# Fences between outputs and crosses: an instruction without operation in place of a copy, one per group in place of two

## The chip, the cores and the metric

The kernel runs on one core of one Trainium2 chip. The metric is the device time in microseconds of one execution, as the median of several runs. The five engines of the core each take their instructions in order from a queue of their own: TensorE (matmuls and weight loads; PE and PEld in the profile), VectorE (DVE), ScalarE (ACT), GpSimd (POOL) and SyncE (SP, which issues DMAs). They wait for each other through semaphores.

## The reference

A retention layer (linear attention with a decay per head) is followed by one wide layer with a swish.

```python
scores = scale * np.matmul(q, k.transpose(0, 1, 3, 2))       # q, k, v: 8 x 8 x 576 x 64, f32
gamma = 1.0 - 2.0 ** (-5.0 - np.arange(H, dtype=np.float32))
Dmat = np.where(rel >= 0, gamma[:, None, None] ** rel[None, :, :], 0.0)
attn = np.matmul(scores * Dmat[None, :, :, :], v)
x = attn.transpose(0, 2, 1, 3).reshape(B * S, H * D)         # 4608 x 512
h = x @ w_in                                                 # w_in: 512 x 2048
out = (h * (1.0 / (1.0 + np.exp(-beta * h)))) @ w_out        # w_out: 2048 x 512
```

## The kernel before

The 576 rows of a batch are cut into 512 rows, in four chunks of 128, and a tail of 64; the eight tails make a ninth block. The retention is computed chunk by chunk: inside a chunk with masked scores (tile `sc`, masked into `R`), across chunks through states (`st`, summed into `sum`, cast into `sbd`/`sbq`, and `end` for the tails). Then the wide layer: `up` (line 775, matmuls into `ph`) and ScalarE's Silu give `gT`; the second product is done as `down` (line 903, `po`) for the first blocks and, from block 3 on, by a scheme of seven products (`seven_mm`, line 811, into `U`, `W`, `Z`). All is placed by hand: `merged` (line 930) walks a list `fill` of matmul steps of the wide layer and puts the steps of the other streams between them, each at a written time.

For batches 2 to 7, the attention output of a batch comes in one group of small matmuls, `both4` (line 707): first `outputs4` (masked scores times values), then `crosses4` (queries times states). The tails have `both_tails` (line 767) with `tail_outputs` and `tail_crosses`. There are seven such groups; in the trace they begin at about 79, 108, 132, 159, 186, 215 and 243 us.

Every small matmul is 64 x 64 with 64 columns of the moving operand. It uses one quarter of the array: a row half (where its operands lie, partitions 0 to 63 or 64 to 127) and a column half (which half of the partitions of the output it writes). The output of a group lies in four PSUM banks, `O4[x, y]`: `x` is the parity of the chunk and the row half that the output matmuls of that bank use, `y` is the pair of heads. `paired` (line 544) issues two lists in step, one for each row half, `j` = 0 and 1.

A cross of row half `j` into a bank `x = j` follows output matmuls of the same row half, and needs no care. A cross of row half `j` into the bank of the other parity would write a bank into which the other row half has been writing; so it must not start before those output matmuls have ended. This is what a fence is for. `fence` (line 555) puts a copy of two columns into ScalarE's queue that waits for the last matmul issued so far, and `mm` (line 549) makes the first cross that is handed the fence wait for that copy; the crosses after it follow in TensorE's queue.

In this kernel a group has two fences: one behind the output matmuls of `y` = 0 and one behind those of `y` = 1. `crosses4` issues, for each row half, first the crosses into the own parity, then in some groups 16 state matmuls of the next batch for each row half (`ahead`; batches 3, 5 and 6), then the crosses into the other parity. In the groups without such states (batches 2, 4 and 7, and the tails) the latter are ordered by `by_banks` (line 663): up to eight for `y` = 0 first, then those for `y` = 1; the first of each waits for its own fence. In batches 3, 5 and 6 they go in turns, `y` = 0, `y` = 1, `y` = 0 and so on. For one batch, row half 0 has 12 crosses into its own parity and 16 into the other, row half 1 has 16 and 12; for the tails it is 16 and 16 for both.

When a group is done, casts (`xT`, line 693, and line 763 for the tails) take the four banks to SBUF.

Of the kernel before, what the change touches and what calls it, by code (L numbers as in the profile page):

```python
# [11 lines left out]
F32 = mybir.dt.float32  # L12
# [7 lines left out]
def kernel(  # L20
# [10 lines left out]
    nc = tc.nc  # L31
# [4 lines left out]
    P = 128  # L36
# [4 lines left out]
    CB = MB // P  # L41
    PC = P // CB
    TL = S - MB
    NT = B // 2
# [16 lines left out]
    consts = ctx.enter_context(tc.tile_pool(name="consts", bufs=1))  # L61
# [86 lines left out]
    lscale = consts.tile([P, 1], F32, name="lscale")  # L148
# [26 lines left out]
    ends = [consts.tile([P, HP, D], BF16, name=f"end{i}") for i in range(B)]  # L175
    sums = [warm[:].rearrange("p (a d) -> p a d", d=D)] + [consts.tile([P, HP, D], F32, name=f"sum{i}")[:] for i in range(3)]
    sbq = [t[:, :, w:w + D] for t in sbds for w in (0, D)] + [consts.tile([P, HP, D], BF16, name="sbq6")[:]]
    fenced = consts.tile([P, 2], F32, name="fenced")
    for s in sbds:
        nc.vector.memset(s[:], 0.0)  # L180

# [105 lines left out]
    def xt(m):  # L287
        if m not in xts:
            xts[m] = xpool.tile([P, HP, CB, P], BF16, name="xT", tag="xT", bufs=2)
        return xts[m]  # L290

    def F(f, *a):
        return lambda: f(*a)  # L293
# [4 lines left out]
    batch, pair, live = {}, {}, {}  # L298
# [118 lines left out]
    def q_cols(i, r, p, kind=None):  # L417

        b, c = seq[i]
        cols = slice(c * PC, (c + 1) * PC) if kind is None else slice(c * PC + kind * PC // 2, c * PC + (kind + 1) * PC // 2)  # L420
        return batch[b]["qT"][r, :, p, cols], lambda o: o.rearrange("k (i s) -> k i s", i=CB)
# [112 lines left out]
    def half(x):  # L534
        return slice(x * TL, (x + 1) * TL)

    def row_d(j):
        return slice(j * D, (j + 1) * D)

    def tile_of(c, kind):  # L540

        return c - c % 2 + (c % 2 if kind else 1 - c % 2)

    def paired(one, two):
        for a, b in zip(one, two, strict=True):
            a()
            b()

    def mm(out, lhsT, rhs, start=False, stop=True, after=None):
        ins = nc.tensor.matmul(out, lhsT, rhs, start=start, stop=stop, skip_group_check=True)  # L550
        if after:
            tc.add_manual_dep(ins.ins, after.pop().ins.name, ordered, reason="row tiles of one bank")
        last[0] = ins

    def fence():
        f = nc.scalar.copy(fenced[:], lscale[:].to_broadcast([P, 2]))
        tc.add_manual_dep(f.ins, last[0].ins.name, ordered, reason="row tiles of one bank")
        return [f]

# [12 lines left out]
    def state_banks(tag="mm"):  # L572
        return [psum.tile([P, 2, HP, D], F32, name="st", tag=t, bufs=dict(mm=3, sc=2, st=1)[t]) for t in (tag, "st")]

    def four_states(b, e, bank):
        return [one_state(b, e + 2 * x, bank[x][:, 0], True) + one_state(b, e + 2 * x + 1, bank[x][:, 1], False)
                for x in range(2)]
# [60 lines left out]
    def new_O4(lead, shape):  # L638
        live[lead]["O4"] = {(x, y): psum.tile(shape, F32, name="O", tag="sc" if x else "O", bufs=2)
                            for x in range(2) for y in range(2)}  # L640
        return live[lead]["O4"]

    def outputs4(b):

        i0 = b * CB
        O4, opened = new_O4(i0, [P, 2, CB, 2 * PC]), set()
        R = batch[b]["R"]

        def one(x, y, cc, pp, kind, hh):
            p, c = 2 * y + pp, 2 * cc + x  # L650
            w = cc * PC + kind * PC // 2
            mm(O4[x, y][row_d(hh), pp, :, w:w + PC // 2], live[i0 + tile_of(c, kind)]["vn"][half(x), 2 * p + hh, :],
               R[cc][half(x), hh ^ y, kind, p, :].rearrange("k (i s) -> k i s", i=CB), start=(x, y, hh) not in opened, stop=False)
            opened.add((x, y, hh))

        after = []
        for y in range(2):
            paired(*[[F(one, x, y, cc, pp, kind, hh ^ x) for cc in range(2) for pp in range(2) for kind in range(2)
                      for hh in range(2)] for x in range(2)])
            after.append(fence())  # L660
        batch[b]["O4"] = O4, after

    def by_banks(items):

        first, second = ([f for z, f in items if z == y] for y in range(2))
        k = min(8, len(first))
        rest = [f for pair in zip(second, first[k:] + [None] * len(second)) for f in pair if f]
        return first[:k] + rest

    def crosses4(b, later=None):  # L670

        i0 = b * CB
        O4, after = batch[b]["O4"]

        def cross(j, e, y, pp, after):
            p, c, kind = 2 * y + pp, e // 2, e % 2
            w = c // 2 * PC + kind * PC // 2
            mm(O4[c % 2, y][row_d(j ^ y), pp, :, w:w + PC // 2], sbq[e - 1][row_d(j), p, :],
               q_cols(i0 + c, row_d(j), p, kind)[0], after=after)

        def crosses(j, x, after=(None, None)):
            items = [(y, F(cross, j, e, y, pp, after[y])) for e in range(1, 2 * CB) if e // 2 % 2 == x for pp in range(2) for y in range(2)]
            return by_banks(items) if x != j and not bank else [f for _, f in items]

        ahead, bank = ([], []), None
        if b < B - 1 and b not in (XB, SB + 1):
            bank = state_banks()
            ahead = four_states(b + 1, 0, bank)
        paired(*[crosses(j, j) + ahead[j] + crosses(j, 1 - j, (None, None) if j else after) for j in range(2)])
        def out(n, x, y, O):  # L690
            to = xt(b)[:, 2 * y:2 * y + 2].rearrange("k p i (c x s) -> k (p i) c x s", c=2, x=2)[:, :, :, x, :]
            e = nc.scalar.copy if n == 1 or b > XB and n % 2 or later is not None else nc.vector.tensor_copy
            e(to, O[:].rearrange("k p i (c s) -> k (p i) c s", c=2))

        outs = [F(out, n, x, y, O) for n, ((x, y), O) in enumerate(O4.items())]
        if later is not None:
            casts = []
            if bank:
                fold(b + 1, 0, bank, casts=casts, by=nc.scalar.copy)
            later += outs + casts  # L700
            return
        for f in outs:
            f()
        if bank:
            fold(b + 1, 0, bank)

    def both4(b, later=None):
        outputs4(b)
        crosses4(b, later)
# [20 lines left out]
    def tail_outputs(i0):  # L730

        O4, opened, R = new_O4(i0, [P, 2, NT, TL]), set(), live[i0]["R"]

        def one(x, y, t, pp, hh):
            p = 2 * y + pp
            mm(O4[x, y][row_d(hh), pp, t, :], live[i0 + t]["vn"][half(x), 2 * p + hh, :],
               R[t // 2][half(x), hh ^ y, t % 2 * HP + p, :], start=(x, y, hh) not in opened, stop=False)
            opened.add((x, y, hh))

        after = []  # L740
        for y in range(2):
            paired(*[[F(one, x, y, t, pp, hh ^ x) for t in range(NT) for pp in range(2) for hh in range(2)]
                     for x in range(2)])
            after.append(fence())
        live[i0]["O4"] = O4, after

    def tail_crosses(i0, later):

        O4, after = live[i0]["O4"]

        def cross(j, x, t, y, pp, after):
            p = 2 * y + pp
            mm(O4[x, y][row_d(j ^ y), pp, t, :], ends[2 * t + x][row_d(j), p, :], live[i0 + t]["qkT"][row_d(j), 0, p, half(x)],
               after=after)

        for own in range(2):
            items = [[(y, F(cross, j, j ^ own, t, y, pp, after[y] if own and not j else None)) for t in range(NT)
                      for pp in range(2) for y in range(2)] for j in range(2)]
            paired(*[by_banks(one) if own else [f for _, f in one] for one in items])
        def out(x, y, O):  # L760
            for r in range(2):
                to = xt(B)[:, 2 * y:2 * y + 2].rearrange("k p (a r) (s l x) -> k (p a) r l x s", r=2, l=2, x=2)[:, :, r, :, x, :]
                nc.scalar.copy(to, O[:].rearrange("k p (a l) (r s) -> k (p a) r l s", l=2, r=2)[:, :, r])

        later += [F(out, x, y, O) for (x, y), O in O4.items()]

    def both_tails(i0, later):
        tail_outputs(i0)
        tail_crosses(i0, later)
# [325 lines left out]
    t = base[2]  # L1095
# [20 lines left out]
    for n in range(SB, B + 1):  # L1116
        t, m = base[n], blocks[n]
        first, second = slice(0, KH // 2), slice(KH // 2, KH)
# [10 lines left out]
    for n in range(1, B):  # L1129
# [3 lines left out]
        b, t = n + 1, base[n]  # L1133
# [20 lines left out]
        else:  # L1154
            rest, outs = [], []
# [39 lines left out]
```

## Time and profile before

| | |
|---|---|
| median of 3 runs | 292.15 us (292.02 to 292.79) |
| the profiled execution | 291.2 us, of which 289.5 us span |
| TensorE busy | 282.9 us (98%), granted clock 0.999 |
| ScalarE busy | 171.9 us (59%) |
| fence copies (L556) | 14, 182 to 193 ns each, first at 79.7, last at 244.4 us |
| all small matmuls | recorded under L550, the helper `mm` |

Since a helper records every small matmul, all of them have line 550; the tile names tell them apart: `O<-R,vn` is an output matmul, `O<-qT,sbd`, `O<-qT,sbq`, `O<-kT,end` and `O<-qT,end` are crosses, `st<-vn,kn` is a state matmul. The start of a matmul's record can be read to the nanosecond, its end is modelled (186 to 240 ns for the small ones), so the pace of the stream is read from start to start. Times of semaphore updates are recorded in the trace too. A few matmul records are missing in some groups.

### The profile page before, as it was taken

How to read it: one execution, taken by the hardware profiler on the slowest of the kernel's cores; microseconds unless marked ns; L12 is line 12 of the kernel's file. 1: busy time of each engine (PE TensorE's matmuls, PEld its weight loads, DVE VectorE, ACT ScalarE, POOL GpSimd, SP SyncE). 2: the span in 40 equal slices, each digit the busy share in tenths (PEclk: the TensorE clock that was granted, in tenths of full speed). 3: DMA queues.
4: the chain of work that ended last, by engine and by line, in shares of the span. 5: the costliest groups of instructions: out<-in, count | busy, mean ns of one | idle time of the engine just before them, and what ended most of it. 6: DMA issues, size and time to landing. Idle time of an engine off the chain costs nothing.

```text
span 289.5 us, 8724 instructions
## 1 busy us (share of the span) xinstructions
PE 282.9 (98%) x3643; PEld 180.0 (62%) x3643; DVE 185.0 (64%) x343; ACT 171.9 (59%) x309; POOL 131.4 (45%) x258
## 2 busy tenths in 40 slices
PE   7899999999999999999999999999999999999995
PEld 5664446874454455468854884578457845784584
DVE  5973545714796288289859855885597455642673
ACT  4367637586968883775357715781576166827730
POOL 7366019934990883295595366533089000000000
PEclk9999999999999999999999999999999999999999
DMA  7999999969999999999998998950779330002004
GB/s 218 309 365 385 381 304 292 187 146 239 184 148 279 242 145 234 285 216 172 217 270 195 154 274 243 200 112 2 226 169 154 81 142 2 2 34 111 2 3 142
DMA packets 120567, 54.05 MB, mean 187 GB/s; under 512 B 93888, under 2 KB 113360, under 8 KB 120528
## 3 DMA queue, kind: packets, MB, share of 16 engines
q1 hardware_dynamic: 120496, 53.49, 78.9%
q8 instruction: 28, 0.46, 0.7%
q14 instruction: 11, 0.09, 0.1%
q10 hardware_dynamic: 32, 0.01, 0.0%
HBM read 36.71 MB, written 9.44 MB: 159 GB/s over the span
## 4 chain that ended last, share of the span: by engine, by line
PE 93%; DMA 3%; DVE 2%; issue 1%; SPq 1%; POOL 0%
PE ph L785 39%; PE po L910 15%; PE U L822 11%; PE Z L822 7%; PE W L822 7%; PE O L550 4%; PE ph L877 4%; DMA kvn<-in_k_dram 3%; PE sc L550 2%; PE st L550 2%; DVE R L448 1%; PE T L414 1%; PE st L510 0%; DVE xT L496 0%; SPq L86 0%
## 5 line engine op out<-in xcount | busy, mean ns | idle before, releaser
L785 PE MATMUL ph<-xT,w_in_sb 128*128 128x512 bf16 (+1 forms) x576 | 116.2, 359 | 0.2 <-DVE xT L496 0.2
L785 PEld LDWEIGHTS <-w_in_sb 128*128 128x128 bf16 x576 | 55.1, 98 | 54.0 <-issue 0.6
L792 ACT ACTIVATE gT<-ph,beta_sb 128x512 bf16<-128x512 f32 (+1 forms) x92 | 58.2, 641 | 39.5 <-PE ph L785 38.8
L822 PEld LDWEIGHTS <-sa 128*128 128x128 bf16 x480 | 46.9, 98 | 5.5
L790 DVE TENSOR_SCALAR gT<-hs,ratio 128x512 bf16<-128x512 f32 x48 | 26.1, 543 | 35.9 <-ACT hs L789 35.6
L330 POOL TENSOR_TENSOR qs<-qn,gq 128x256 bf16<-128x256 f32 x48 | 29.0, 636 | 32.9 <-DMA qn<-in_q_dram 29.2
L789 ACT ACTIVATE hs<-ph,beta_sb 128x512 f32<-128x512 f32 x48 | 33.0, 687 | 18.2 <-PE ph L785 18.0
L910 PE MATMUL po<-w_out_sb,gT 128*128 128x512 bf16 x192 | 43.3, 379 | 0.0
L806 DVE TENSOR_TENSOR sa<-gT 128x1024 bf16<-128x1024 bf16 (+1 forms) x54 | 41.4, 808 | 1.1 <-PE Z L822 0.9
L312 POOL TENSOR_TENSOR vn<-kvn,gv 128x256 bf16<-128x256 f32 x48 | 33.3, 715 | 3.4 <-issue 2.2
L367 POOL CAST kn<-kvn 128x128 bf16<-128x128 f32 (+1 forms) x72 | 26.6, 406 | 15.4 <-DMA kvn<-in_k_dram 15.4
L910 PEld LDWEIGHTS <-gT 128*128 128x128 bf16 x192 | 18.1, 98 | 20.8
L822 PE MATMUL Z<-b,sa 128*128 128x256 bf16 x192 | 22.9, 273 | 0.0
L822 PE MATMUL U<-b,sa 128*128 128x256 bf16 x192 | 22.9, 273 | 0.0
L293 DVE TENSOR_TENSOR R<-sc,late 128x512 bf16<-128x512 f32 x24 | 15.4, 680 | 11.2 <-issue 10.0
L822 PEld LDWEIGHTS <-gT 128*128 128x128 bf16 x192 | 18.7, 98 | 3.3
L255 DVE TENSOR_TENSOR b<-wt 128x512 bf16<-128x512 f32 x20 | 16.3, 872 | 1.9 <-ACT wt L238 1.8
L448 DVE TENSOR_TENSOR R<-sc,causal 128x512 bf16<-128x512 f32 x16 | 10.2, 683 | 2.1 <-PE sc L550 1.8
L822 PE MATMUL W<-b,gT 128*128 128x256 bf16 x96 | 11.5, 273 | 0.0
L822 PE MATMUL W<-b,sa 128*128 128x256 bf16 x96 | 11.5, 273 | 0.0
L822 PE MATMUL U<-b,gT 128*128 128x256 bf16 x96 | 11.5, 273 | 0.0
L379 POOL CAST kn<-kvn 128x512 bf16<-128x512 f32 x6 | 3.8, 653 | 16.0 <-DMA kvn<-in_k_dram 16.0
(121 smaller groups left out, 322.5 us busy)
## 6 DMA issues: line engine op xcount, KB each, us to landing
qn<-in_q_dram SPq DMA_DIRECT2D x16, 512.0 KB, 5.6
out_dram<-ot SPq DMA_DIRECT2D x32, 256.0 KB, 3.1
wt<-in_moe_w_out_dram SPq DMA_DIRECT2D x8, 512.0 KB, 9.4
kvn<-in_k_dram SPq DMA_DIRECT2D x12, 256.0 KB, 6.0
kvn<-in_v_dram SPq DMA_DIRECT2D x12, 256.0 KB, 6.1
kvn<-in_k_dram SPq DMA_DIRECT2D x24, 128.0 KB, 4.4
kvn<-in_v_dram SPq DMA_DIRECT2D x24, 128.0 KB, 4.0
wt<-in_moe_w_in_dram SPq DMA_DIRECT2D x5, 512.0 KB, 9.7
```

Of the source, the lines that this page charges most:

```text
L255: nc.vector.tensor_tensor(to, x, y, op)
L312: nc.gpsimd.tensor_tensor(vn[:, hs], v[:, hs], g[:, hs], ALU.mult)
L330: nc.gpsimd.tensor_tensor(batch[b]["qs"][:, cs, to], q_tiles[b][:, hs, cs].rearrange("p h i d -> p i h d"), gq[:, cs, hs].unsqueeze(3).to_ ...
L367: nc.gpsimd.tensor_copy(kn[:, c % 2, to], t[:, 0, hs])
L550: ins = nc.tensor.matmul(out, lhsT, rhs, start=start, stop=stop, skip_group_check=True)
L785: nc.tensor.matmul(ph[:, cs], w_in_sb[:, ko, fo * P:(fo + 1) * P], xts[m][:, ko, cs, w], start=(ko == 0 and n == 0), stop=(ko == KO - 1), ...
L789: nc.scalar.activation(h, ph, ACT.Silu, scale=beta_sb[:, fo:fo + 1])
L790: nc.vector.tensor_scalar(gts[m][:, fo], h, ratio[:, fo // 2:fo // 2 + 1], None, ALU.mult)
L792: nc.scalar.activation(gts[m][:, fo, :, w], ph, ACT.Silu, scale=beta_sb[:, fo:fo + 1])
L806: nc.vector.tensor_tensor(sums_a[0][:, held_in[j], ks], quarter(m, *x, ks), quarter(m, *y, ks), op)
L822: nc.tensor.matmul(chains[c, n][:, 0 if alone else p], a, sevens[k // 2][:, j - 1, k % 2, :], start=j in (3, 4, 1) and k == 0 and (alone o ...
L910: nc.tensor.matmul(po[:, :nn], gT[:, fo, ms, :], w_out_sb[:, fo, n0:n0 + nn], start=(fo == 0), stop=(fo == FO - 1))
```

## The change

`fence` emits an instruction without operation in place of the copy, and the two-column tile `fenced` goes. A group has one fence, behind the output matmuls of both `y`. `by_banks` goes: the crosses into the other parity are issued in turns in all groups, and the first of row half 0 waits for the one fence. Own-parity crosses, states and casts stay as they are, in the same order.

```diff
     def fence():
-        f = nc.scalar.copy(fenced[:], lscale[:].to_broadcast([P, 2]))
+        f = nc.scalar.nop()
         tc.add_manual_dep(f.ins, last[0].ins.name, ordered, reason="row tiles of one bank")
         return [f]
...
-        after = []
         for y in range(2):
             paired(*[[F(one, x, y, cc, pp, kind, hh ^ x) for cc in range(2) for pp in range(2) for kind in range(2)
                       for hh in range(2)] for x in range(2)])
-            after.append(fence())
-        batch[b]["O4"] = O4, after
-
-    def by_banks(items):
-
-        first, second = ([f for z, f in items if z == y] for y in range(2))
-        k = min(8, len(first))
-        rest = [f for pair in zip(second, first[k:] + [None] * len(second)) for f in pair if f]
-        return first[:k] + rest
+        batch[b]["O4"] = O4, fence()
...
-        def crosses(j, x, after=(None, None)):
-            items = [(y, F(cross, j, e, y, pp, after[y])) for e in range(1, 2 * CB) if e // 2 % 2 == x for pp in range(2) for y in range(2)]
-            return by_banks(items) if x != j and not bank else [f for _, f in items]
+        def crosses(j, x, after=None):
+            return [F(cross, j, e, y, pp, after) for e in range(1, 2 * CB) if e // 2 % 2 == x for pp in range(2) for y in range(2)]
...
-        paired(*[crosses(j, j) + ahead[j] + crosses(j, 1 - j, (None, None) if j else after) for j in range(2)])
+        paired(*[crosses(j, j) + ahead[j] + crosses(j, 1 - j, None if j else after) for j in range(2)])
...
         for own in range(2):
-            items = [[(y, F(cross, j, j ^ own, t, y, pp, after[y] if own and not j else None)) for t in range(NT)
-                      for pp in range(2) for y in range(2)] for j in range(2)]
-            paired(*[by_banks(one) if own else [f for _, f in one] for one in items])
+            paired(*[[F(cross, j, j ^ own, t, y, pp, after if own and not j else None) for t in range(NT) for pp in range(2)
+                      for y in range(2)] for j in range(2)])
```

The tails' `tail_outputs` changes as `outputs4` does.

More of the change, by code (lines that the diff above doesn't have):

```diff
@@ L177 @@
     sbq = [t[:, :, w:w + D] for t in sbds for w in (0, D)] + [consts.tile([P, HP, D], BF16, name="sbq6")[:]]
-    fenced = consts.tile([P, 2], F32, name="fenced")
     for s in sbds:
@@ L738, in one @@
             opened.add((x, y, hh))
-        after = []
         for y in range(2):
@@ L743, in tail_outputs @@
                      for x in range(2)])
-            after.append(fence())
-        live[i0]["O4"] = O4, after
+        live[i0]["O4"] = O4, fence()
     def tail_crosses(i0, later):
```

## The prediction

> **What bounds the kernel now.** I read the page's busy shares first, then the clock row, then the chain that ended last, and from there went into single groups with the timeline of TensorE.
>
> ```profile
> PE 282.9 (98%) x3643; PEld 180.0 (62%) x3643; DVE 185.0 (64%) x343; ACT 171.9 (59%) x309; POOL 131.4 (45%) x258
> ...
> PEclk9999999999999999999999999999999999999999
> ...
> PE 93%; DMA 3%; DVE 2%; issue 1%; SPq 1%; POOL 0%
> ```
>
> TensorE is busy 98% of the span, at full clock, and the chain is 93% TensorE. The time-ordered chain from 200 to 250 us holds nothing but TensorE pieces, the two groups of outputs and crosses in it among them:
>
> ```profile
> 215.09 1.59 PE O L550 x120
> 216.68 2.70 PE ph L785 x12
> ...
> 243.60 1.52 PE O L550 x126
> 245.12 2.69 PE ph L785 x12
> ```
>
> So 0.1 us taken out of one of the seven groups is 0.1 us off the end. ScalarE's saved instructions (14 copies of 0.19 us, 2.7 us together, and seven waits beside them) are off the chain and count nothing by themselves; what hides them is TensorE's own work, and ScalarE would have to grow by tens of us to show.
>
> The last group, the tails, shows both prices that matter. Columns are start, length, instruction and count:
>
> ```profile
> 244.06 0.34 PE L550 MATMUL O<-kT,end 64*64 64x64 bf16 x16
> 244.21 0.32 PE L550 MATMUL O<-qT,end 64*64 64x64 bf16 x16
> ...
> 244.46 0.31 PE L550 MATMUL O<-kT,end 64*64 64x64 bf16 x8
> 244.60 0.26 PE L550 MATMUL O<-qT,end 64*64 64x64 bf16 x6
> 244.68 0.22 PE L550 MATMUL O<-kT,end 64*64 64x64 bf16 x2
> 244.70 0.20 PE L550 MATMUL O<-qT,end 64*64 64x64 bf16 x2
> 244.73 0.26 PE L550 MATMUL O<-kT,end 64*64 64x64 bf16 x6
> 244.83 0.29 PE L550 MATMUL O<-qT,end 64*64 64x64 bf16 x8
> 245.05 0.39 PE L785 MATMUL ph<-xT,w_in_sb 128*128 128x512 bf16 x1
> ```
>
> The first 32 crosses (both halves of the rows on their own banks, outputs y = 0 and 1 in turns) start between 244.06 and 244.35. Then TensorE stands for 0.10 us until the first fence. The 32 crosses behind the fences start between 244.46 and 244.93: 0.47 us for as many matmuls. One matmul's record is 0.19 us long, so a block's last start lies 0.19 before its end.
>
> **Why the crosses behind the fence are slow.** In the single records the first 32 start 8.3 ns apart, those behind the fence in pairs: 3 ns, then 28 ns. A 64x64 matmul on one quarter of the array returns every 31.7 ns. In turns, the stream uses all four quarters (row half j, column half j^y), so one starts every 8 ns; bank by bank, both row halves work on one y, two quarters only, so one starts every 15.8 ns. The same holds at the other three groups ordered bank by bank (b = 2, 4, 7): one row half's eight crosses of y = 0 at 79 us fill 80.11 to 80.36, its eight of y = 1 fill 80.51 to 80.75. In the groups b = 3, 5, 6, which are in turns already, the crosses behind the fence start 8.3 ns apart (187.39 to 187.59).
>
> **What a fence takes.** From the trace's semaphore updates around the second fence of the group at 79 us: TensorE's update at 80.186, ScalarE's separate wait instruction (17 ns long) starts at 80.207, the copy at 80.264, ScalarE's update comes at 80.465, the waiting weight load starts at 80.506. That is 21 + 57 + 201 + 41 = 320 ns from TensorE's update to TensorE going on. The pair of copies in the timeline of ScalarE (the bracket is the idle time before it and what ended it):
>
> ```profile
> 79.73 0.19 ACT L556 COPY fenced<-lscale 128x2 f32<-128x2 f32 x1
> 80.26 0.19 ACT L556 COPY fenced<-lscale 128x2 f32<-128x2 f32 x1 [0.34 <-PE O L550]
> ```
>
> **The change, part by part.**
>
> Copy to instruction without operation. No row of before shows one with a wait and an update. Nearest are the semaphore instructions: they start 17 to 28 ns after the update they wait for (ScalarE's 21), last 17, and one of GpSimd's that only updates starts at 0.679 with its update at 0.704, 25 ns. I take 21 + 25 + 41 = 87 ns from update to TensorE. Below, it cannot beat 21 + 41 = 62 ns; above, I take the copy's whole 320. A second wait in front of it would add the 57 ns seen above. I take 87, since all three parts are rows of sequencer instructions.
>
> One fence per group. The first waiting cross now waits for the last output matmul, not for the last of y = 0. The last output's update comes at 80.186, 133.130, 215.926 and 244.309 in the four bank-by-bank groups, and TensorE runs out of free crosses at 80.13, 133.07, 215.79 and 244.36. With 87 ns it goes on at 80.273, 133.217, 216.013 and 244.396: stalls of 0.14, 0.14, 0.22 and 0.04 us. Before, the stalls were 0.14 (80.36 to 80.51, at the second fence), 0.14 (133.30 to 133.45), 0.15 + 0.05 (at both, since ScalarE's copy started only after an activation) and 0.10. Waiting earlier therefore costs nearly nothing here, because the fence is quicker by 233 ns.
>
> All crosses in turns. After the release 32 crosses remain, starting over 31 x 8.35 = 0.259 us (rate of the 26 last crosses at 109.749 to 109.966). The next wide matmul starts 144 ns after the last cross where four quarters were in use (109.966 to 110.110), 125 ns where two were (80.751 to 80.876). So the next matmul comes at update + 0.087 + 0.002 + 0.259 + 0.144 = 0.492 us. Before it came at update + 0.690 in the three groups (80.186 to 80.876, 133.130 to 133.819, 215.926 to 216.615) and + 0.743 in the tails (244.309 to 245.052). Gains: 3 x 0.198 + 0.251 = 0.845 us. Bounds: if the pace stayed at 15.8 ns, the term is update + 0.087 + 0.002 + 31 x 0.0158 + 0.125 = 0.704, and the sum over the four is +0.00 us; if the pace comes and the fence takes 320 ns, 0.233 x 4 = 0.93 is lost again, +0.09; both together, +0.93.
>
> The three groups in turns already. There 32 state matmuls lie in front of the waiting cross. At 109 us the second fence's load started at 109.625, 41 ns after ScalarE's update, and the matmuls show some 0.03 us of wait; at 160 and 187 us none. I take -0.03 in all; what covers the fence is those states (0.25 us), and a fence up to 0.29 us after the update stays hidden (160.046 against 159.755).
>
> One update fewer on TensorE. The last output of y = 0 no longer posts one. In the records a matmul 32 places behind a posting one starts 39 ns after the post (79.707 and 79.746), 18 ns behind its neighbour instead of 8: 10 ns x 7 = -0.07 us. The Trainium skill, "TensorE: Matmul & The Clock Gate", section "The cost: per-tile semaphore tail", puts each increment at 26.3 ns; by it this term would be 7 x 0.026 = -0.18 us (an estimate), and the trace, where two neighbouring posts lie 34 ns apart (80.152 and 80.186), does not exclude it.
>
> Evacuations and queues. The banks of y = 0 now fill at the end, together with y = 1. The first copy out of them starts at 81.01 at b = 2, after the last cross, and at 133.74 at b = 4, behind the second fence's crosses; the new last crosses come at 80.53 and 133.48, and a post takes 0.23 more, so nothing gets later. Behind the fence in ScalarE's queue stand waits and activations that start 1.5 us later at b = 5 to the tails (161.55 at b = 5); at most one decode is lost. No DMA, SP or POOL instruction is touched.
>
> Sum: -0.845 - 0.03 - 0.07 = -0.95 us. The profiled execution took 291.2 (289.5 of span and 1.7 around it), so 290.25 by its own time; it lies 0.95 under the median of the runs shown, 292.15, which I use: 292.15 - 0.95 = 291.2 us, 0.33% less. About 0.3%, 0.88 us, is what a measurement of this kernel can tell from no change.
>
> **Rivals.**
>
> A, the pace does not come. The alternation is between column halves, and if only the two row halves could overlap, the crosses would stay at 15.8 ns: 292.15 + 0.00 - 0.10 = 292.05, same. For it: the crosses behind the fence are the only evidence at b = 2, 4, 7. Against: the crosses ahead of the fence, same shape, run at 8.3 ns in each of these groups. The Trainium skill, same page, section "The mechanism", says that a weight load overlaps matmuls in flight only where their row group differs, which would make the column alternation useless and gives this rival's time. The trace disagrees in its 8.3 ns.
>
> B, the fence is no quicker. If the wait is met but the post comes as late as the copy's (a second wait and a drain of the queue before it): 0.233 x 4 lost, 292.15 + 0.09 - 0.10 = 292.1, same. Against it are the 17 ns rows.
>
> C, slower: the release comes only when an activation ends. If the instruction's post is tied to its neighbour in the queue, TensorE waits 0.021 + 0.69 (an activation) + 0.041 = 0.75 us after the update. Four groups lose 0.75 - 0.087 = 0.66 each against the forecast, the three covered ones 0.75 - 0.29 = 0.46: 4.0 - 0.95 = +3.1 us, 295.2. The kernel is slower by over 0.3% from a release 0.44 us after the update on. Against: ScalarE's wait instruction at 244.33 started while a copy was still running (244.22 to 244.41), so such instructions are not tied to the engine.
>
> D, more gain: posts of the last outputs also come 0.03 to 0.1 us earlier with one update fewer (latency from start to post: 0.25 us in the tails, 0.33 at b = 3, 0.44 at b = 2 and 4): another 0.3, 290.9.
>
> **How the numbers follow.** Forecast 0.58, A 0.12, B 0.12, C 0.08, D 0.10. The forecast's own spread is 290.9 to 291.6 (the 57 ns of a second wait four times are 0.23 above; the runs of before span 0.8), and three fifths of it lie below 291.27, the bound of faster: 0.36, with D 0.46. Same: 0.22 + A and B 0.20 in all nearly, 0.43. Slower: C and the rest of A and B with both failing (293.0), 0.11. The range reaches down to 290.8 (D) and up to 292.3 (A and B).
>
> **What would show it.** Right: no copies on line 556's place; the crosses behind the fence start some 8 ns apart in all seven groups; from the last output's update to the next wide matmul 0.49 us instead of 0.69; each of the four O groups of the chain 0.2 us shorter. Wrong: crosses still paired at 31 ns (A), a release over 0.2 us after the update (B), or stalls in the groups b = 3, 5, 6 as well (C).

## The result, and the profile after

The changed kernel takes 290.96 us in the median of 15 runs (290.21 to 291.46), the kernel before 291.87 us in as many runs beside it (291.19 to 292.79). The ratio is 0.9968 with a 95% interval of 0.9958 to 0.9978, or -0.93 us (-1.23 to -0.64). The forecast was 291.2 us against a median of 292.15, so -0.95; the absolute time came out 0.24 us lower because the kernel before is 0.28 us lower over 15 runs than over the three shown ahead.

The page of the changed kernel, its profiled execution at 290.9 us with 289.2 us of span (busy time by engine; TensorE's granted clock in 40 slices; the chain that ended last):

```profile
PE 281.4 (97%) x3643; PEld 178.1 (62%) x3643; DVE 185.3 (64%) x343; ACT 169.7 (59%) x295; POOL 134.7 (47%) x258
...
PEclk9999999999999999999999999999999999999999
...
PE 93%; DMA 3%; DVE 1%; issue 1%; SPq 1%; ACT 0%; POOL 0%; ACTq 0%
```

Nothing changed in kind: TensorE is the bound, at full clock, 1.5 us less busy. ScalarE has 14 instructions fewer and lost 2.2 us. New is a trace of ACTq, ScalarE's instruction queue: the fence is no longer work of the engine. The chain in order of time, 200 to 250 us (start, length, what):

```profile
215.30 0.82 PE O L549 x64
216.12 0.02 issue
216.15 0.02 ACTq L555
216.17 0.04 issue
216.21 0.45 PE O L549 x32
216.66 2.70 PE ph L771 x12
...
243.57 1.22 PE O L549 x128
244.79 2.70 PE ph L771 x12
```

Batch 7 (215 us) took 1.59 us before and takes 1.36 now; the tails (243 us) took 1.52 and take 1.22. In batch 7 the fence itself stands on the chain in three short pieces, 0.02 + 0.02 + 0.04 us, and the 32 crosses behind it with their drain take 0.45.

The fence in the trace, all seven of them, 17 ns each, and ScalarE's engine around the last one:

```profile
L555 ACTq EVENT_SEMAPHORE  x7: 17/17/17, 80.4 to 244.3; - x7
```

```profile
243.61 0.69 ACT L778 ACTIVATE gT<-ph,beta_sb 128x512 bf16<-128x512 f32 x1 [0.17 <-PE ph L771]
```

The seventh starts at 244.279 us and posts at 244.302, while this activation runs to 244.301. That is too near its end to tell whether a fence has to wait for an activation; the third experiment tells. In all seven groups the fence starts 21 or 22 ns after TensorE's update. TensorE's timeline of the tails:

```profile
243.72 0.50 PE L549 MATMUL O<-R,vn 64*64 64x64 bf16 x40
244.03 0.32 PE L549 MATMUL O<-kT,end 64*64 64x64 bf16 x16
244.16 0.32 PE L549 MATMUL O<-qT,end 64*64 64x64 bf16 x16
244.35 0.32 PE L549 MATMUL O<-kT,end 64*64 64x64 bf16 x16
244.49 0.30 PE L549 MATMUL O<-qT,end 64*64 64x64 bf16 x16
244.72 0.61 PE L771 MATMUL ph<-xT,w_in_sb 128*128 128x512 bf16 x2
```

The last two lines of crosses are the ones behind the fence. They start within 0.25 us where the kernel before needed 0.47, and they no longer fall into pieces of eight and two.

Not all of the gain in the groups reaches the end of this execution. From the first to the last small matmul the seven groups are 1.15 us shorter than before, but the stretches between them are 0.59 us longer. Four of these seven stretches differ from before by 5 ns or less and one by 40 ns. The other two are longer by 0.11 us (behind batch 4) and 0.45 us (behind batch 5). In the second, TensorE waits for VectorE at 178.72 us; the list of waits puts 0.2 us of it down to that, and VectorE's timeline shows what was late:

```profile
PE ph L771 <- DVE sum L585: 0.2, 1, 0.2
```

```profile
177.20 1.26 DVE L776 TENSOR_SCALAR gT<-hs,ratio 128x512 bf16<-128x512 f32 x1 [2.83 <-ACT hs L775]
178.38 0.41 DVE L585 TENSOR_TENSOR warm<-sum,st 128x256 f32<-128x256 f32 x1
```

In the profile of before that TENSOR_SCALAR took 0.49 us and the next instruction began at 177.70.

The stretch ahead of the first group, which the change doesn't touch, is 0.23 us longer here too. So the two profiled spans differ by 0.31 us only (289.49 and 289.18), and the size of the gain is read from the medians, not from this pair of profiles.

### The profile page after: what moved, and what is told of

Same layout as the page of the kernel before. It is cut to its first block, busy times and chain, and to the rows that moved or that the text cites. A ratio compares the mean times of both kernels' runs of the same rounds, so it can differ in the third digit from the quotient of the medians.

```text
span 289.2 us, 8713 instructions
## 1 busy us (share of the span) xinstructions
PE 281.4 (97%) x3643; PEld 178.1 (62%) x3643; DVE 185.3 (64%) x343; ACT 169.7 (59%) x295; POOL 134.7 (47%) x258
## 4 chain that ended last, share of the span: by engine, by line
PE 93%; DMA 3%; DVE 1%; issue 1%; SPq 1%; ACT 0%; POOL 0%; ACTq 0%
PE ph L771 39%; PE po L896 15%; PE U L808 11%; PE Z L808 7%; PE W L808 7%; PE O L549 4%; PE ph L863 4%; DMA kvn<-in_k_dram 3%; PE sc L549 2%; PE st L549 2%; PE ph L878 1%; PE O L476 1%; PE st L509 1%; PE T L413 0%; DVE gT L776 0%
## 5 line engine op out<-in xcount | busy, mean ns | idle before, releaser
L329 POOL TENSOR_TENSOR qs<-qn,gq 128x256 bf16<-128x256 f32 x48 | 30.1, 659 | 31.4 <-DMA qn<-in_q_dram 21.7
L792 DVE TENSOR_TENSOR sa<-gT 128x1024 bf16<-128x1024 bf16 (+1 forms) x54 | 42.9, 834 | 1.4 <-PE Z L808 1.2
L311 POOL TENSOR_TENSOR vn<-kvn,gv 128x256 bf16<-128x256 f32 x48 | 35.2, 757 | 2.2 <-DMA kvn<-in_v_dram 1.7
L682 ACT CAST xT<-O 128x512 bf16<-128x512 f32 x19 | 9.8, 599 | 5.7 <-PE O L549 5.7
```

What stands on the lines that cost most here:

```text
L311: nc.gpsimd.tensor_tensor(vn[:, hs], v[:, hs], g[:, hs], ALU.mult)
L329: nc.gpsimd.tensor_tensor(batch[b]["qs"][:, cs, to], q_tiles[b][:, hs, cs].rearrange("p h i d -> p i h d"), gq[:, cs, hs].unsqueeze(3).to_ ...
L792: nc.vector.tensor_tensor(sums_a[0][:, held_in[j], ks], quarter(m, *x, ks), quarter(m, *y, ks), op)
```

## The experiments

All times are against the kernel before on the same chip; a difference in us is the ratio less one, times that median (291.58 us in the first set of four, 291.68 in the second, 291.9 for the last run). By the theory of the prediction two prices add: the release of the fence, and the pace of the crosses behind it. The rivals are that one of the two does nothing, or that it works only together with the other.

### One copy as the fence, in turns

```diff
 # the changed kernel, with the copy back
     def fence():
-        f = nc.scalar.nop()
+        f = nc.scalar.copy(fenced[:], lscale[:].to_broadcast([P, 2]))   # and the tile fenced, as before
```

> The changed kernel with the copy put back as the one fence of each group; order in turns. Theory of two terms (a release 0.233 us quicker, and a pace of 8.3 ns behind it in place of 15.8): the next wide matmul comes 0.320 + 0.41 = 0.73 us after the last output's update, against 0.69 before and 0.50 in the changed kernel, so 291.9 us beside a kernel before of 291.9: +0.0 (-0.1 to +0.2). Rival 'order alone' (the kind of the fence is hidden): as the changed kernel, -0.9. Rival 'kind alone' (the order of the crosses is worth nothing): about +0.1 as well, so this run speaks only against the first rival.

Measured: 291.02 us, ratio 0.9983 (0.9972 to 0.9994), -0.50 us (-0.82 to -0.17). That is more gain than the theory allowed. The chain at batch 4:

```profile
132.53 0.76 PE O L550 x64
133.29 0.02 issue
133.31 0.20 ACT fenced L556
133.51 0.04 issue
133.55 0.44 PE O L550 x32
134.00 1.85 PE W L809 x16
```

The crosses behind the fence run at the fast pace (32 starts in 252 ns) with the copy too, so the pace belongs to the order alone. The theory had 0.73 us from the update to the next wide matmul; each of the four groups has 0.644. Of the difference 55 ns are the release and some 30 ns the crosses and the drain behind them. This and the update that is gone make -0.30 us, which is also by how much the seven groups are shorter in this profile; -0.30 lies within the measured interval. A single copy releases in 22 + 201 + 42 = 265 ns, not in the prediction's 320, because a separate wait is missing. Before, the second copy of a group wrote the same tile `fenced` as the first and waited for it as well as for TensorE, which took an instruction of its own ahead of it (80.207, the copy at 80.264). A lone copy has no such wait: it starts 22 ns after the update (80.433 and 80.455).

### One fence without operation, crosses bank by bank

```diff
 # the kernel before
-        f = nc.scalar.copy(fenced[:], lscale[:].to_broadcast([P, 2]))
+        f = nc.scalar.nop()
...
-            after.append(fence())
-        batch[b]["O4"] = O4, after
+        batch[b]["O4"] = O4, fence()      # one per group, also in the tails
...                                       # crosses: `after` in place of `after[y]`; by_banks stays
```

> The changed kernel with the crosses bank by bank again in batches 2, 4, 7 and the tails; one fence without operation per group. Theory of two terms: release 0.087 us after the update, then 32 crosses at 15.8 ns, the next wide matmul 0.70 us after the update: -0.15 us against before (-0.3 to +0.1). Rival 'kind alone': as the changed kernel, -0.9. Rival 'order alone': 0.0.

Measured: 291.38 us, ratio 0.9990 (0.9981 to 0.9998), -0.29 us (-0.55 to -0.06). The kind and number of the fence alone give a third of the gain, as the two-term theory has it. Its tails, the crosses behind the fence:

```profile
244.12 0.31 PE L549 MATMUL O<-kT,end 64*64 64x64 bf16 x8
244.27 0.20 PE L549 MATMUL O<-qT,end 64*64 64x64 bf16 x2
244.28 0.22 PE L549 MATMUL O<-kT,end 64*64 64x64 bf16 x2
...
244.43 0.29 PE L549 MATMUL O<-qT,end 64*64 64x64 bf16 x8
```

They start over 0.40 us, where the prediction's 15.8 ns for each would make 0.49. The single starts show why. Within one bank pair they come in pairs 31 ns apart. At the switch from y = 0 to y = 1 (244.25 to 244.37) they come in fours, since the two quarters of y = 1 are free while those of y = 0 still work. Before, the second fence kept the two mostly apart.

### Both fences without operation, everything else as before

```diff
 # the kernel before, two fences per group, bank by bank
     def fence():
-        f = nc.scalar.copy(fenced[:], lscale[:].to_broadcast([P, 2]))
+        f = nc.scalar.nop()
```

> The kernel before with both its copies replaced by instructions without operation, two fences per group, bank by bank. Theory of two terms: the crosses of y = 0 go on without a stall and the release of y = 1 comes before they are through, so nothing is waited for at all, but the pace is 15.8 ns: -0.13, -0.14, -0.20 and -0.09 in the four groups and -0.03 elsewhere, -0.6 us against before (-0.4 to -0.75). Rival 'order alone': 0.0. Rival 'kind alone': -0.9 or more.

Measured: 291.08 us, ratio 0.9981 (0.9968 to 0.9994), -0.55 us (-0.93 to -0.17), as expected. TensorE has no stall at any fence of batches 2, 4, 7 and the tails in its trace. With two early releases the bank order costs no stall, but it still spreads the 32 last crosses over 0.38 to 0.49 us.

This trace also shows that the fence doesn't wait for an activation of its engine (rival C). ScalarE in the tails:

```profile
244.86 0.69 ACT L791 ACTIVATE gT<-ph,beta_sb 128x512 bf16<-128x512 f32 x1 [0.17 <-PE ph L784]
```

The first of the two fences starts at 245.256 us, 21 ns after TensorE's update, and posts its own at 245.280, while the activation runs to 245.54. In batches 5, 6 and 7 it is the same: a start 0.29 us before the end of an activation, and the post 24 ns later.

### Two copies in a row as the fence, in turns

```diff
 # the kernel with one copy, in turns
         f = nc.scalar.copy(fenced[:], lscale[:].to_broadcast([P, 2]))
+        f = nc.scalar.copy(fenced[:], fenced[:])
```

> One fence per group made of two copies, the second waiting for the first; order in turns. It doubles the price of the fence: release some 0.57 us after the update. If every ns of a late release in the four bank-by-bank groups goes to the end, and groups 3, 5 and 6 are covered up to 0.29 us: 4 x 0.25 + 3 x 0.25 = +1.75 us against the run with one copy (+1.4 to +2.0). If the release is hidden by other work: 0.0. If only the four groups count: +1.0.

Measured: 292.29 us, ratio 1.0019 (1.0007 to 1.0032), +0.55 us, so +1.05 by the ratios and +1.27 by the medians against one copy, below the +1.4 to +2.0 that was expected. The chain at batch 4:

```profile
133.78 0.02 issue
133.80 0.20 ACT fenced L556
134.00 0.02 issue
134.03 0.20 ACT fenced L558
134.23 0.04 issue
134.27 0.45 PE O L550 x32
134.72 1.31 PE W L810 x11
```

A copy more on the way is 223 ns, and it comes out one to one: the groups of batches 2, 4 and the tails are 0.22 us longer than with one copy, that of batch 7 0.11 (its update came 0.12 us sooner after the last output, 0.263 against 0.382). The groups with states ahead (3, 5, 6) lost only 0.06 to 0.10 us, less than the theory took: their states cover more of the fence than I had given them. The sum over the groups is +1.00 us. That it is the figure of the rival that counts the four uncovered groups alone is chance: 0.78 us of it comes from those four and 0.22 from the three others.

### One copy, bank by bank

```diff
 # the kernel before
-            after.append(fence())
-        batch[b]["O4"] = O4, after
+        batch[b]["O4"] = O4, fence()      # one copy per group, also in the tails
...                                       # crosses: `after` in place of `after[y]`; by_banks stays
```

> The kernel before with one copy as the fence of a group instead of two, crosses bank by bank as before: the corner that is missing between two fences, kinds and orders. By the two-term theory both prices add. From the copy in turns (291.02 us) only the pace is lost: 4 groups x (31 x 7.45 ns - 19 ns of shorter drain) = 0.85 us, 291.9 us, some 0.3 over the kernel before. From the single fence without operation, bank by bank (291.38 us), the copy's 0.233 x 4 = 0.93 comes on top: 292.3 us, +0.7. So +0.3 to +0.7, and stalls of 0.33 us in front of the waiting cross at batches 2 and 4. The rival, that the kind of the fence counts only together with the order, expects no change (within 0.2 us of before).

Measured: 291.95 us, ratio 1.0005 (0.9990 to 1.0020), +0.15 us (-0.29 to +0.58). The time alone can't tell +0.3 from nothing. The chain at batch 4 can:

```profile
133.60 0.02 issue
133.62 0.20 ACT fenced L556
133.82 0.04 issue
133.87 0.59 PE O L550 x31
134.46 1.63 PE W L818 x14
```

The copy costs what it costs in turns (0.02 + 0.20 + 0.04), and the crosses what they cost with the other fence, 0.59 us against 0.44 in turns. The prices add. With one fence the four corners by the ratios are:

| | bank by bank | in turns | order is worth |
|---|---|---|---|
| copy | +0.15 us | -0.50 us | 0.65 us |
| without operation | -0.29 us | -0.93 us | 0.64 us |
| kind is worth | 0.44 us | 0.43 us | |

Each entry is uncertain by 0.3 to 0.4 us, so the agreement of the two columns is closer than it need be. One fence alone, as a copy, brings nothing.

The traces give the two prices more sharply. From the last output's update to the next wide matmul, at batch 4, in ns:

| kernel | measured | release + first cross + crosses + drain |
|---|---|---|
| before, two copies, by banks | 689 | 320, the second copy; then half of the crosses |
| one copy, by banks | 792 | 265 + 2 + 400 + 125 |
| one copy, in turns | 644 | 265 + 2 + 252 + 125 |
| two copies in a row, in turns | 867 | 488 + 2 + 252 + 125 |
| one without operation, by banks | 613 | 87 + 2 + 399 + 125 |
| the changed kernel | 466 | 87 + 2 + 252 + 125 |

So a group in which TensorE waits at the fence gains 178 ns by the kind of the fence and 147 ns by the order. Over four groups that is 0.71 and 0.59 us, and the times have 0.44 and 0.65; within their uncertainty the two agree.

### The changed kernel again

> The changed kernel as it is, so that it stands on the same chip as the runs beside it. The theory of the prediction (a quicker release, and four quarters of the array behind it) gives 0.95 us under the kernel before, with +/-0.3. Its seven groups should again be about 1.1 us shorter together than before's 13.42 us. A second thing is asked of its profile: in the first one TensorE stood 0.36 us at 178.72 us for a late addition of VectorE. If that comes again, the change itself causes a new wait there; if it is gone, it was one execution's accident.

Measured: 290.95 us, ratio 0.9969 (0.9950 to 0.9988), -0.90 us. From first to last small matmul its groups are 1.18 us shorter than before's, as in the first profile (1.15). The wait at 178 us is gone, and its stretch is as before to 1 ns. Instead the stretch behind batch 4 is 0.33 us longer, and that behind batch 6 0.21 us. Behind batch 4:

```profile
PE U L808 <- DVE ot L822: 0.2, 1, 0.2
```

TensorE waits here for VectorE, which is behind with the sums `sa`: the seven of L792 take 5.61 us in this execution; in the profile of before the same seven (L806) took 4.67. Behind batch 6, at 189.95 us, TensorE waits for a sum of line 585 again. So none of these waits comes with every execution of the changed kernel, but both executions met some: all seven stretches together are 0.59 us longer than before in the first and 0.57 in the second. In the profiles of the first four experiments they are 0.02 to 0.29 us longer.

### The instruction in TensorE's own queue

```diff
 # the changed kernel
-        f = nc.scalar.nop()
+        f = nc.tensor.nop()
```

> The changed kernel with its instruction without operation in TensorE's own queue instead of ScalarE's. No second engine is asked, so a theory that counts hops alone expects a quicker release: 41 ns less in four groups, -0.16 us against the changed kernel. The theory that the crosses between the outputs and the fence are what hides the post of the last output expects it slower: TensorE now stands at the fence before those 28 to 64 matmuls, in all seven groups, until the update comes 0.24 to 0.38 us after the last output's start. With 45 ns from the update to the next matmul, 8.35 ns for each of the 60, 64 or 92 matmuls left, and 144 ns to the wide one, the next wide matmul comes 0.68, 0.72 and 0.95 us after the update, where the changed kernel has 0.47 to 0.50 (60 or 64 left) and 0.75 to 0.82 (92 left): 0.186 + 0.197 + 0.216 + 0.134 + 0.142 + 0.216 + 0.249 = +1.34 us against the changed kernel (+1.1 to +1.6), no reading of line 555 later than 25 ns after the update, and no stall further down in any group.

Measured: 292.50 us, ratio 1.0025 (1.0006 to 1.0044), +0.73 us, 1.63 us slower than the changed kernel, where +1.34 (+1.6 at most) was expected. The chain at batch 4:

```profile
133.48 0.85 PE O L549 x64
134.33 0.14 issue
134.46 0.64 PE O L549 x56
```

TensorE stands after the outputs: 450 to 581 ns from the last output to the next small matmul in batches 2 to 7, 373 in the tails. In the changed kernel 24 to 32 crosses, and in three groups states too, start in that time. So the crosses ahead of the fence are the cover, and an engine of its own for the fence is what lets them run. The release wasn't the 45 ns I took, though: the instruction starts 28 ns after the update and lasts 51 ns on this queue, and the first matmul behind it starts 136 ns after the update, later than by way of ScalarE (88).

### The instruction in SyncE's queue

```diff
 # the changed kernel
-        f = nc.scalar.nop()
+        f = nc.sync.nop()
```

> The changed kernel with its instruction without operation in SyncE's queue. If only the kind of the instruction counts, it equals the changed kernel. If what is queued ahead on the fence's engine counts, it is much slower: in the order of SyncE's queue the fence stands behind DMA issues which in the changed kernel's profile end at 88.6, 119.8, 139.8, 163.2, 186.2 and 219.4 us, while the fences are needed at 80.4, 109.4, 133.0, 159.5, 187.2 and 216.1 us. Taken singly that is 8.2 + 10.4 + 6.8 + 3.7 + 0 + 3.3 us; since a TensorE that stands lets the queue of DMAs catch up, the sum of 32 us is an upper bound, and I take 8 us (the first wait alone) as the lower one.

Measured: 313.91 us, ratio 1.0747 (1.0710 to 1.0785), +21.8 us. SyncE's timeline around the first group, and who waited for line 555:

```profile
81.85 2.67 SPq L389 DMA_TRANSPOSE qT<-qs  x2
84.62 1.27 SPq L389 DMA_TRANSPOSE kT<-kn  x1
85.94 2.06 SPq L887 DMA_DIRECT2D out_dram<-ot  x4
88.21 1.51 SPq L389 DMA_TRANSPOSE kT<-kn  x1
```

```profile
L555 SPq EVENT_SEMAPHORE  x7: 17/17/17, 88.1 to 267.1; - x7
...
  PE O L549: 16.6, 3
```

The instruction is the same 17 ns, but it comes up only behind four DMA issues at 88.1 us. TensorE stands 7.41, 6.45 and 3.30 us in front of the waiting cross in batches 2, 3 and 7 (8.2, 10.4 and 3.3 expected when taken singly) and hardly at all in the others. That is 17.2 us; nearly all of the rest goes with the clock. The row of TensorE's granted clock in this kernel's page:

```profile
PEclk9999999999859999599999999999997999999999
```

During each of the three waits the granted clock falls to 0.5, and it stays there when the matmuls go on: for 10.2 us from 83.6 us, for 6.8 us from 124.6 us and for 3.4 us from 237.2 us. The stretches behind these three groups are 2.59, 2.29 and 1.26 us longer than before's, the others as before to 1 ns. What is queued ahead of a fence on its engine is its price here, and a long wait costs clock on top.

### Outputs ordered by pair of chunks

```diff
 # the changed kernel, outputs4
-        for y in range(2):
-            paired(*[[F(one, x, y, cc, pp, kind, hh ^ x) for cc in range(2) for pp in range(2) for kind in range(2)
+        for cc in range(2):
+            paired(*[[F(one, x, y, cc, pp, kind, hh ^ x) for y in range(2) for pp in range(2) for kind in range(2)
                       for hh in range(2)] for x in range(2)])
```

> The changed kernel with the output matmuls of a batch ordered by pair of chunks first and y second, instead of y first. The two outputs that post an update in the middle of the last 18 (places 46 and 47 of 64, the last readers of one mask tile) then stand at places 30 and 31. The theory that posts shortly ahead of the last one delay it expects the last output's update 0.24 to 0.28 us after its start in batches 2 to 6 (the tails, with one post alone, have 0.237; batches 2 to 6 have 0.315 in undisturbed groups), the stall at the fence of batches 2 and 4 down from 0.15 to about 0.11 us, and the next wide matmul still 0.466 us after the update: 0.12 us in all, 290.8 us, less than the times can tell from the changed kernel. The rival, that 0.315 is what the update of a pair takes, expects 0.315 again and no change.

Measured: 290.79 us, ratio 0.9967 (0.9955 to 0.9979), -0.96 us: the same as the changed kernel within 0.3 us. The mechanism is as expected: the last output's update comes 0.279 us after its start in batches 2, 4 and 5, where the changed kernel has 0.315 when undisturbed (batches 3 and 6 have 0.38 and 0.36 here). But the last output starts 35 ns later. A matmul 32 places behind one that posts an update waits for that post: in batch 4 the matmuls at places 62 and 63 start 40 and 39 ns after the posts of 30 and 31. With the posts at places 30 and 31 of 64 this pause falls on the last two outputs, where it fell on crosses before. From the last output's start to the next wide matmul batch 4 takes 751 ns instead of 781, and from the start of the group nothing is won.

## Why the prediction was right

**The path.** TensorE's own time in the groups was the bound (93% of the chain again), and ScalarE's 2.2 us stood off the chain (0%). That 0.1 us out of a group is 0.1 us off the end, as the prediction said without a condition, held only where no other wait came up: waits on VectorE took back up to 0.45 us at one place.

**The release.** Forecast 21 + 25 + 41 = 87 ns from update to weight load; measured 22 + 23 + 42 = 87 (update 80.410, instruction 80.432, its own update 80.455, load 80.497), and 86 at batch 4 (132.966 to 133.052). The stall at the fence is 0.15 us at batches 2 and 4 (forecast 0.14), 0.24 at batch 7 (0.22) and 0.05 in the tails (0.04).

**The comparison price of the copy was wrong.** The bound "if the pace comes and the fence takes 320 ns, +0.09" took the price of the second copy of a pair for that of any copy. A lone copy takes 265 ns, and the kernel with it came out 0.50 us faster.

**The pace.** Forecast 8.35 ns a cross and 0.144 us of drain; measured 252 to 265 ns for 31 steps, 8.1 to 8.5 ns, and 0.125 us of drain in three of the four groups. Coming out of a stall the crosses fall into fours (three steps of 3 ns and one of 22), and after them the wide matmul follows sooner. So from update to wide matmul 0.496, 0.466, 0.466 and 0.466 us against a forecast of 0.492. By these the term of the four groups is (0.690 - 0.496) + 2 x (0.690 - 0.466) + (0.743 - 0.466) = 0.92 us; the forecast had 0.845. The pace of the bank order, 15.8 ns, was right for two fences, and too slow for one, where the switch between banks overlaps (0.40 us).

**The update that is gone.** 10 ns for each group was read off before's records. The last output now starts 9 ns sooner after the wide matmul ahead of the group (0.825 us against 0.834, 0.718 against 0.726), -0.06 us in all. The 26.3 ns for each increment of the Trainium skill ("TensorE: Matmul & The Clock Gate", section "The cost: per-tile semaphore tail") would make 0.18 us, an estimate; these traces don't bear it out.

**The covered groups.** Forecast -0.03 us for batches 3, 5 and 6. From wide matmul to wide matmul they changed by -0.08, +0.11 and -0.06 us, together -0.03 in the first profile, where pauses of 0.12 us lie in two of them; so the agreement is chance. No stall stands at their fences.

**The rivals.** A falls: four quarters run at 8.1 ns behind the fence too. The sentence of the Trainium skill ("TensorE: Matmul & The Clock Gate", section "The mechanism") that weight loads overlap matmuls in flight only where the row group differs doesn't hold for these 64 x 64 tiles. B falls with the 87 ns. C falls with the kernel of two fences without operation, where four fences post 0.26 us before the end of an activation. The Trainium skill ("PSUM — Partial Sum Buffer", section "Engine vs sequencer instructions") calls a nop an instruction of the sequencer alone, and that trace agrees. D is half right, for another reason than it gave: at batches 2 and 4 the updates came 0.34 and 0.32 us after the last output instead of 0.44, but because pauses that are no part of the kernel's waits (below) were shorter or absent.

**The total.** The forecast -0.95 us and the measured -0.93 agree better than their parts. The groups gained 1.15 us in the profile, more than forecast, through the shorter drain and through pauses that before's profile happened to have. On the other side stand the longer stretches between the groups, which the forecast didn't have: 0.6 us in each of the two profiled executions, the larger part of it waits on VectorE. A larger gain in the groups and longer stretches between them, neither of them in the forecast, work against each other, so that the total fits so closely is in part luck. How much of the longer stretches belongs to an average execution can't be read from single profiles.

## What to carry to other kernels

A fence that only passes a wait on needs no work: an instruction without operation on another engine took 87 ns from update to release, a small copy 265, and a second copy into the same tile 320. Choose the engine by what is ahead in its queue (behind SyncE's DMA issues it made the kernel 22 us slower, some 6 us of it by the lower clock) and let it be another engine than the one that waits (in TensorE's own queue it cost 1.6 us), so that what doesn't need the fence can run in the meantime. Where small matmuls use quarters of the array, order them so that all quarters are in use behind a wait, and price a step by the update and the next start rather than by the records' lengths.

## What the runs showed that I had not expected

TensorE's dense stretches of small matmuls have pauses of 0.08 to 0.13 us, in single cases 0.2 to 0.4, with no semaphore wait on the instruction that follows. They come at other places in each profile: at 79.88, 109.64, 132.76 and 187.17 us before, at 79.96, 159.75 and 187.46 in the changed kernel's first profile, at 80.87 (234 ns) and 110.00 in its second, at 110.75 (379 ns) in the kernel with reordered outputs. Since two executions of one kernel differ in them, they are tied neither to the fences nor to a place in the instruction stream; their cause stays open. They put 0.1 us of chance on the length of a group in one profile, so a term of this size has to be taken from several groups or several kernels.

The VectorE sum `sa` of 128x1024 elements, on which the wait behind batch 4 hangs, has no fixed length. In the eleven profiles 302 of these sums ran with no GpSimd record beside them, and all took 0.68 or 0.69 us. 151 ran with GpSimd busy for more than 95% of their time, and 140 of those took 0.77 to 1.10 us. The TENSOR_SCALAR of 1.26 us in the first profile ran from 177.20 us beside two GpSimd products that lasted until 178.18; that of 0.49 us before met only the last 0.18 us of one. I read this off the timelines only; no run was made to separate it.

Waits on VectorE stand in the profiles of all kernels whose fence on ScalarE has no operation: besides the two of the changed kernel, 0.72 us behind batch 4 with the reordered outputs, and 0.23 us behind batch 2, for a cast of the group's output, in both kernels that go bank by bank. In the profiles of before, of the three kernels with copies and of the one with the fence in TensorE's queue no stretch is more than 0.06 us longer than before's. That fits a TensorE that gains time in the groups and then catches up with VectorE, but no run tests it.
